# Low weight bits joined as words, bonus rows, copies from two queues, three output tiles: a linear-attention and feed-forward kernel on one core

## Chip, cores, metric

One core of one Trainium2 chip. The metric is the device time of one execution in microseconds (us); the median of three runs of the kernel before is 497.73 us (496.38 to 502.05).

## The reference, cut to what matters

```
# r, k, v: (4, 8, 768, 48);  w, u: (8, 48)
for t in range(768):                       # per batch and head
    y[t]  = r[t] @ (state + outer(u * k[t], v[t]))
    state = w[:, None] * state + outer(k[t], v[t])
x = y, heads side by side                  # 3072 tokens x 384
h = x @ w_in                               # 384 x 2048
out = (h * clip(h + 3, 0, 6) / 6) @ w_out  # 2048 x 384
```

All is float32. The term with `u` (the bonus) acts only between a token and itself.

## The kernel before, in words

The tokens go in chunks of 64 (`C`), with 12 chunks (`NSTEP`) and two halves of the batch-and-head pairs per chunk, so 24 attention steps `i` (`NHALF`). Six groups `g` (`NG`) of 512 columns each hold four attention steps: steps 0 to 3 feed group 0, 4 to 7 group 1, and so on. The feed-forward part runs per group over 16 slices `f` of the hidden width. A unit is one (group, f). Its first half (`ffn1`, line 484; the nine products of `hidden`, line 190) makes a 128x512 tile `h`, which ACT and DVE turn into the activated tile `g` as a high and a low part. Its second half (`ffn2`, line 511; nine products of `project`, line 197) adds to three output banks `o`. Every weight is a pair `w_hi`, `w_lo`, because a product is made of three products of rounded parts.

One attention step (`attention`, line 443) loads `kT`, `rT`, `kt`, `V`, scales keys and queries with powers of `w` (`prepare`: `ks`, `RP`; for steps under `EARLY` = 8 also the elementwise product `X` = `ks` * `RP`), makes the 64x64 scores on PE (`scores`, line 365), puts the bonus on the diagonal of `X` (`put`, line 418) and the masked scores under it (`copy_predicated`, line 441), then on PE the state update (`keep`) and the outputs (`outputs`). A `visit` (line 400) is one block of such small PE products. The state goes through `St` (DVE, line 464) and back into the bank `U` (ACT, line 456). The outputs are split into `x` high (ACT, line 471) and `x` low (DVE, line 472); where a chunk's second half is done, six copies of 32 KB inside on-chip memory (line 479) complete the rows of `x`. Before the change all six are issued by SP.

In steps under 8 the bonus is a product with one column per pair (`self_weight`, line 371): 16 products with `uw` as the single right-hand column, written to column 0 of each score block. `put` then spreads that column over the row. Steps 1 and 3 use output banks 1 and 2 in place of `SC` and `Y` (`where`, line 247). Steps under `APART` have a score visit of their own; later ones share the visit of the step before.

The weights come as 64-bit words (`weights`, line 275), three loads per f into two `raw` buffers in turn. Per f: the upper word is scaled into `z` (line 289 on ACT or 290 on DVE), the low word is rounded by ACT into the low 16 bits of the upper word, in place (line 292, uint32 to uint16, strided), DVE masks sign and three low bits from it (line 293), shifts and joins with `z` (line 295), rounds to `w_hi` (297 ACT or 298 DVE) and subtracts to `w_lo` (line 259).

The three output banks are slices of one tile `ops3`. All instruction orders come from a list scheduler written in the kernel (`Schedule`, line 58): every operation has a cost per engine, its reads and writes by name, and a priority from the longest path behind it; `order` (line 82) picks engine and time. `products` (line 119) also plans instruction fetch in blocks of 256 PE products (`FETCH` us each) and fills idle PE time with products of no use (`warm`, line 615; line 619 in the profile). The constants at lines 41 to 55 are its costs. Engines run their instructions strictly in the emitted order, and the real waits between engines are set from the accesses to tiles. Units go in the order: group 0 f 0 to 5 (`SPLIT`), group 1 whole, group 0 f 6 to 15, groups 2 to 5 whole. The first `CUT` units of group 0 are cut into halves of 256 columns, one per chunk. After group 0's first six, ACT saves the banks to `part` (line 542).

The pages of the profile name fp32 weight loads PEld. `idc` is a 64x64 identity, twice over; `ident` a 128x128 one.

Of the kernel before, what the change touches and what calls it, by code (L numbers as in the profile page):

```python
# [13 lines left out]
U16 = mybir.dt.uint16  # L14
# [27 lines left out]
BEGIN = {"pe": 1.4, "act": 2.1, "dve": 0.9, "pool": 0.8, "sp": 0.8}  # L42
ISSUE, FLIGHT = 0.47, 1.95
QUEUE = 0.3
PIECES = 3
BLOCK, FETCH, FIRST = 256, 4.4, 63
# [3 lines left out]
APART = 5  # L50
SPLIT = 6
LAG = 2
CUT = 1
AHEAD = 4
XBUF = (0, 1, 1, 0, 1, 0)


class Schedule:
# [23 lines left out]
    def order(self):  # L82
# [23 lines left out]

        def run(state, start, count, pace):

            seen, entered = state
            while count:  # L110
                room = BLOCK - seen % BLOCK
                if count < room:
                    return (seen + count, entered), start + count * pace
                start = entered = max(start + room * pace, entered + FETCH)
                seen += room
                count -= room
            return (seen, entered), start

        def products(i, start):

            nonlocal pe
            gap = start - free["pe"] - 0.2
            pace = ops[i][0]["pe"] / ops[i][6]
            busy = [d for d, h in holds.items() if h is None or h + 0.3 > free["pe"]]
            choices = [0]
            if gap > 0.3 and not busy:
                choices = range(int(gap / 0.87) + 1, max(int(gap / 0.87) + 2, int(gap / 0.125)))
            best = None
            for c in choices:
                state, t = run(pe, free["pe"], 4 * c, gap / (4 * c)) if c else (pe, start)  # L130
                state, t = run(state, max(start, t), ops[i][6], pace)
                room = BLOCK - state[0] % BLOCK
                wait = max(0.0, state[1] + FETCH - t - 0.008 * room)
                score = (round(t + 0.5 * wait, 2), c)
                if best is None or score < best[0]:
                    best = score, c, state, t
            _, c, pe, t = best
            if c:
                fills.append((free["pe"] + 0.02, c, gap / c))
            if ops[i][7] is not None:  # L140
                holds[ops[i][7]] = None
            return t
# [3 lines left out]
        while ready:  # L146
            best = None
            for e in free:
                here = [i for i in ready if e in ops[i][0]]
                if not here:  # L150
                    continue
                t = min(begin(i, e) for i in here) + 0.1
                for i in sorted((i for i in here if begin(i, e) <= t), key=lambda i: -prio[i]):
                    start = begin(i, e)
                    end = start + (ISSUE if e == "sp" else ops[i][0][e])
                    if any(begin(i, x) + c < end for x, c in ops[i][0].items() if x != e):
# [6 lines left out]
            if e == "sp":  # L163
                free[e] = start + ISSUE
                line = ready_at = max(line, start + FLIGHT) + ops[i][0][e]
            elif e == "pe":
                free[e] = ready_at = products(i, start)
            else:
                free[e] = ready_at = start + ops[i][0][e]
            if e in ops[i][4]:  # L170
                port = free[e]
            if i in holds:
                holds[i] = free[e]
            done.append((start, free[e], e, i))
            for j in succ[i]:
                for x in at[j]:
                    at[j][x] = max(at[j][x], ready_at + (WAIT[e] if x != e or e == "sp" else 0.03)
                                   + (SPARE.get(e, 0.0) if x != e and ops[j][5] else 0.0))
                waits[j] -= 1
                if not waits[j]:  # L180
                    ready.append(j)
# [22 lines left out]
def fast_path(tc, mp, pp, sb, w_hi, w_lo, b3, wm, badi, hps, ops3, rT, kT, rt, kt, vt, wp, wu, wcat, out):  # L204
# [40 lines left out]
    ops = [ops3[:, m] for m in range(3)]  # L245
# [17 lines left out]
    def load(i):  # L263
        q = i % 2
        for name, dst, src, cost in (("kT", kTt, kT, 0.86), ("rT", rTt, rT, 0.86), ("V", V, vt, 0.74),
# [3 lines left out]
            S.add({"sp": cost}, [], [(name, q)], lambda e, dst=dst, src=src: dma(dst[q], src[i]), LEAD)  # L269
# [5 lines left out]
    def weights(f):  # L275
        for p in range(PIECES):
            cs = slice(NW // PIECES * p, NW // PIECES * (p + 1))
            S.add({"sp": 2.2 / PIECES}, [], [("raw", f % 2, p)], lambda e, cs=cs: dma(raw[f % 2][:, cs], wcat[f][:, cs]))
        words = "p (n two) -> p n two"
        rw, zf, sg = raw[f % 2], z[f % 2], cv[f % 2]  # L280
# [4 lines left out]
        up_b = rw.bitcast(U16).rearrange("p (n four) -> p n four", four=4)[:, :, 2]  # L285
# [6 lines left out]
        S.add({"act": 1.2}, [], [kr + (p,) for p in range(PIECES)], lambda e: act.mul(out=up_b, in_=low, mul=ROUND))  # L292
        S.add({"dve": 0.47}, [kr + (p,) for p in range(PIECES)], [kc], lambda e: dve.tensor_scalar(
            out=sg, in0=up_i, scalar1=-2 ** 31 + 7, scalar2=None, op0=ALU.bitwise_and), port=True)
        S.add({"dve": 0.87}, [kz, kc], [kz], lambda e: dve.scalar_tensor_tensor(  # L295
            out=zi, in0=zi, scalar=3, in1=sg, op0=ALU.logical_shift_left, op1=ALU.bitwise_or), port=True)
# [5 lines left out]
    def consts():  # L302
        def init_pool(e):
            make_identity(nc, ident)
# [5 lines left out]
        S.add({"pool": 1.6}, [], ["ident", "idc"], init_pool, 200)  # L310
# [6 lines left out]
        S.add({"act": 1.0}, ["ident"], ["idc", "mask"], init_mask)  # L317
# [12 lines left out]
        S.add({"pe": 3.1}, ["ident"], ["Y", "o2", "U"], init_rows, 300, count=12)  # L330
# [33 lines left out]
    def scores(i):  # L364
# [8 lines left out]
        work = [score] + [self_weight] * (i < EARLY)  # L373
        return [[functools.partial(fn, n, k) for n in range(2)] for fn in work for k in range(8)], \
            [("ks", q), ("RP", q)] + [("X", q), "uw"] * (i < EARLY), [key]
# [23 lines left out]
    def visit(down, across):  # L399
# [12 lines left out]
        S.add({"pe": 0.25 + 0.11 * max(map(len, one_side))}, list(dict.fromkeys(reads)), list(dict.fromkeys(writes)),  # L412
# [4 lines left out]
    def put(i, bonus, e):  # L417
        eng[e].tensor_tensor(out=X[i % 2], in0=wide(idc), in1=bonus.unsqueeze(2).broadcast_to([128, 8, C]), op=ALU.mult)  # L418
# [17 lines left out]
    def choose(i):  # L436
        q = i % 2
        sc, key = where(i)[0], where(i)[2]
        if i < EARLY:
# [3 lines left out]
    def attention(i):  # L443
# [5 lines left out]
        if i < APART:  # L449
            prepare(i)  # L450
            visit([scores(i)], [])
# [22 lines left out]
        if hf == 1:  # L474
            for n in range(2):
                for j in range(3):
                    r0, d0 = 64 * n + 16 * j, 64 * n + 48
                    S.add({"sp": 0.12}, [("x", XBUF[g], c, b, hl) for b in range(2) for hl in range(2)],
                          [("xh", XBUF[g], c, n, j)], lambda e, j=j, r0=r0, d0=d0: dma(
# [132 lines left out]

    done, fill = S.order()
# [14 lines left out]
def rwkv_ffn_kernel(ctx: ExitStack, tc: tile.TileContext, rT, kT, rt, kt, vt, wp, wu, wcat, ys, out):  # L628
# [13 lines left out]
    ops3 = pp.tile([128, 3, 512], F32, name="o")  # L642
    ops = [ops3[:, m] for m in range(3)]

    with tc.tile_pool(name="main", bufs=1) as mp, tc.manual_schedule():
        fast_path(tc, mp, pp, sb, w_hi, w_lo, b3, wm, badi, hps, ops3, rT, kT, rt, kt, vt, wp, wu, wcat, out)
# [135 lines left out]
```

## Time and profile before

| what | us |
|---|---|
| median of three runs | 497.73 |
| lowest and highest | 496.38, 502.05 |
| the profiled execution, its own time | 497.16 |
| its span, first to last instruction | 495.4 |

The span is 1.76 us shorter than the execution's time. The profile is of one execution. Engines are PE (matrix products), PEld (its weight loads), DVE, ACT, POOL; SPq is the queue engine that issues DMAs. In a list by time each row has its start, its duration, engine, line, tiles and, in brackets, how long the engine was idle before and who released it. The granted clock is a share of full speed.

### The profile page before, as it was taken

The page shows a single profiled execution, that of the slowest core. Times are in us where ns is not written, and L with a number is a line of the kernel's source. Part 1 is how long each engine was busy: PE and PEld are TensorE (multiplying, and loading weights), DVE is VectorE, ACT ScalarE, POOL GpSimd, SP SyncE. Part 2 cuts the span into 40 slices and gives each one's busy share as a digit, 9 for nine tenths or more (in the row PEclk, how much of TensorE's full clock was granted, in tenths as well). Part 3 has the DMA queues.
Part 4 walks back from the last instruction along what each step waited for, and adds up shares of the span by engine and source line. Part 5 has one row for each costly group of instructions (what it writes and reads, how often), then busy time and mean ns, then how long its engine had stood idle before and what let it go on. Part 6 is the DMA issues. An engine that isn't in the chain of part 4 may idle for free.

```text
span 495.4 us, 11559 instructions
## 1 busy us (share of the span) xinstructions
PE 475.2 (96%) x4994; PEld 389.9 (79%) x4994; DVE 295.5 (60%) x475; ACT 197.7 (40%) x289; POOL 38.3 (8%) x40
## 2 busy tenths in 40 slices
PE   8977999799999999999999999999999999999993
PEld 5776877688888888888888788888788888888882
DVE  6786997998574686743566543685543652333331
ACT  2145777787334333333323433343433332433331
POOL 1411310000000111100010000120000100000000
PEclk9887999999999999999999999999999999999998
DMA  8768655456112143330033410143400010100001
GB/s 207 225 168 242 188 154 185 149 179 190 33 53 99 52 121 100 112 110 0 16 115 91 140 28 0 54 129 92 132 3 1 17 34 17 64 1 0 2 0 69
DMA packets 27516, 44.28 MB, mean 89 GB/s; under 512 B 4161, under 2 KB 12482, under 8 KB 27458
## 3 DMA queue, kind: packets, MB, share of 16 engines
q1 hardware_dynamic: 27458, 43.47, 29.5%
q8 instruction: 41, 0.67, 0.6%
q14 instruction: 17, 0.14, 0.1%
HBM read 36.38 MB, written 4.72 MB: 83 GB/s over the span
## 4 chain that ended last, share of the span: by engine, by line
PE 92%; DVE 3%; DMA 2%; issue 1%; ACT 0%; SPq 0%; POOL 0%; DVEq 0%; POOLq 0%
PE o L200 40%; PE h L193 39%; PE Y L362 5%; PE SC L362 2%; PE h L619 2%; PE U L362 2%; PE o L362 1%; DMA x<-x 1%; DMA raw<-wcat 1%; DVE w_lo L259 0%; DVE z L295 0%; PE Y L328 0%; PE o L328 0%; DVE X L418 0%; DVE x L472 0%
## 5 line engine op out<-in xcount | busy, mean ns | idle before, releaser
L200 PE MATMUL o<-g,w_hi 128*128 128x512 f32 (+1 forms) x582 | 195.1, 390 | 4.0 <-ACT part L542 3.2
L193 PE MATMUL h<-x,w_hi 128*128 128x512 f32 (+1 forms) x582 | 164.9, 392 | 4.0 <-DVE t L500 4.0
L500 DVE SCALAR_TENSOR_TENSOR t<-t,h 128x512 f32<-128x512 f32 (+1 forms) x97 | 66.1, 681 | 113.0 <-ACT t L498 112.8
L200 PEld LDWEIGHTS o<-g,w_hi 128*128 128x128 f32 x582 | 108.9, 188 | 29.3 <-ACT part L542 3.7
L193 PEld LDWEIGHTS h<-x,w_hi 128*128 128x128 f32 x582 | 108.1, 188 | 27.2 <-DVE t L500 4.7
L498 ACT ACTIVATE t<-h,b 128x512 f32<-128x512 f32 (+1 forms) x97 | 66.5, 685 | 147.3 <-PE h L193 146.7
L200 PE MATMUL o<-g,w_lo 128*128 128x512 f32 (+1 forms) x291 | 112.7, 387 | 0.0
L259 DVE TENSOR_TENSOR g<-t,g 128x512 fp32r<-128x512 f32 (+1 forms) x97 | 66.4, 685 | 43.2 <-ACT g L504 43.1
L504 ACT CAST g<-t 128x512 fp32r<-128x512 f32 (+1 forms) x97 | 60.3, 621 | 73.4 <-DVE t L500 73.4
L193 PE MATMUL h<-x,w_lo 128*128 128x512 f32 (+1 forms) x291 | 82.0, 390 | 0.0
L193 PEld LDWEIGHTS h<-x,w_lo 128*128 128x128 f32 x291 | 54.6, 189 | 11.7 <-DVE w_lo L259 0.3
L200 PEld LDWEIGHTS o<-g,w_lo 128*128 128x128 f32 x291 | 54.7, 188 | 10.7
L259 POOL TENSOR_TENSOR RP<-rT,E 112x512 f32<-112x512 f32 x16 | 20.2, 1265 | 298.6 <-PE Y L362 272.8
L292 ACT ACTIVATE raw<-raw 128x768 uint16<-128x768 uint32 x16 | 31.3, 1957 | 5.0 <-DVE z L290 4.7
L362 PEld LDWEIGHTS U<-V,KH 64*48 64x48 f32 x704 | 19.1, 128 | 9.5 <-issue 8.3
L362 PE MATMUL SC<-RP,ks 48*64 48x64 f32 x704 | 26.0, 224 | 0.1
L362 PE MATMUL Y<-X,V 64*48 64x64 f32 x704 | 25.7, 226 | 0.0
L362 PEld LDWEIGHTS SC<-RP,ks 48*64 48x64 f32 x704 | 23.1, 137 | 1.7 <-issue 0.6
L362 PE MATMUL U<-V,KH 64*48 64x48 f32 x704 | 21.9, 215 | 2.6 <-issue 1.6
L362 PE MATMUL Y<-RP,St 48*48 48x64 f32 x672 | 24.4, 224 | 0.0
L471 ACT CAST x<-Y 112x512 fp32r<-112x512 f32 x22 | 12.9, 584 | 27.8 <-PE Y L362 27.8
L362 PEld LDWEIGHTS Y<-X,V 64*48 64x48 f32 x704 | 23.2, 128 | 0.0
(83 smaller groups left out, 308.8 us busy)
## 6 DMA issues: line engine op xcount, KB each, us to landing
raw<-wcat SPq DMA_DIRECT2D x48, 256.0 KB, 3.4
kT<-kT SPq DMA_DIRECT2D x24, 224.0 KB, 4.6
rT<-rT SPq DMA_DIRECT2D x24, 224.0 KB, 4.3
kt<-kt SPq DMA_DIRECT2D x24, 192.0 KB, 4.6
V<-vt SPq DMA_DIRECT2D x24, 192.0 KB, 3.2
rt<-rt SPq DMA_DIRECT2D x16, 192.0 KB, 4.5
outT<-cv SPq DMA_DIRECT2D x12, 256.0 KB, 2.1
x<-x SPq DMA_DIRECT2D x72, 32.0 KB, 2.0
```

The costliest lines, as they stand in the source:

```text
L193: nc.tensor.matmul(h, (w_hi, w_lo)[wl][:, f, 0, 128 * j:128 * j + 128], x(j, hl), start=(m == 0 and j == 0), stop=(m == 2 and j == 2))
L200: nc.tensor.matmul(o[m], (w_hi, w_lo)[wl][:, f, 1, 128 * m:128 * m + 128], g(hl), start=(clear and k == 0), stop=(last and k == 2), skip_g ...
L259: emit = lambda e: eng[e].tensor_tensor(out=out, in0=in0, in1=in1, op=op)
L292: S.add({"act": 1.2}, [], [kr + (p,) for p in range(PIECES)], lambda e: act.mul(out=up_b, in_=low, mul=ROUND))
L362: nc.tensor.matmul(out, lhsT, rhs, start=start, stop=True, skip_group_check=True)
L471: S.add({"act": 0.49}, [ky], [kx + (0,)], lambda e: act.copy(out=hi, in_=yt), LEAD)
L498: S.add({"act": 0.13 + 0.23 * ns}, [("h", n % 2), "b3"], [kt_], lambda e: act.activation(out=t[:, :T], in_=h[:, :T], func=AF.Relu, bias=b3 ...
L500: last = S.add({"dve": 0.05 + 0.28 * ns}, [("h", n % 2), kt_], [kt_], lambda e: dve.scalar_tensor_tensor(out=t[:, :T], in0=t[:, :T], scala ...
L504: S.add({"act": 0.08 + 0.22 * ns}, [kt_], [kg + (0,)], lambda e: act.copy(out=gt[:, 0, :T], in_=t[:, :T]))
L619: nc.tensor.matmul(hps[1][:, :cols], ident, rhs, start=True, stop=True)
```

## The change

1. Weights: ACT writes the rounded low word to a separate int32 tile (`cv`, now called `bits`), contiguous. DVE joins sign bit and low bits in one two-input instruction, in place of the one-input mask; the shift and join into `z` follows as before. The planned costs are 0.82 (ACT) for 1.2, and 0.87 (DVE) for 0.47.
2. Bonus in steps 0 to 3: four products per half with `uw` broadcast as 64 weight columns and 128 columns of `X`, into a bank of their own (`h0` for even, `o0` for odd steps); `put` multiplies that bank with the identity. Steps 4 to 7 keep the one-column form.
3. The 12 copies of `x` of group 0 may be issued by ACT or SP, as the scheduler chooses.
4. The scheduler leaves 0.6 us behind a run of fill products (0.2 before), counts them at double length before 7 us, and fetch at 4.9 us per block up to 50 us and 3.9 after (4.4 before). Planned DMA costs rise a little.
5. The output banks are three tiles.
6. `APART` is 4 (5), `CUT` is 2 (1). The set-up of `ident` and `idc` is two operations, `ident` first; the first row products are planned at 5.0 us (3.1).

```
-BEGIN = {"pe": 1.4, ...}
-ISSUE, FLIGHT = 0.47, 1.95
+BEGIN = {"pe": 1.45, ...}
+ISSUE, ISSUE_ACT, FLIGHT = 0.47, 0.65, 1.95
-BLOCK, FETCH, FIRST = 256, 4.4, 63
+BLOCK, FETCH, DENSE, FIRST = 256, (4.9, 3.9), 50.0, 63
+COLD, SLACK = 7.0, 0.6
-APART = 5
+APART = 4
-CUT = 1
+CUT = 2
...
-            gap = start - free["pe"] - 0.2
+            gap = start - free["pe"] - SLACK
+            wide = 1.74 if start < COLD else 0.87
...
+    def bonus_bank(i):
+        bank, key = ((hps[0], ("h", 0)), (ops[0], "o0"))[i % 2]
+        return bank.rearrange("s (k t) -> s k t", t=C), key
...
-        S.add({"act": 1.2}, [], [kr + (p,) ...], lambda e: act.mul(out=up_b, in_=low, mul=ROUND))
-        S.add({"dve": 0.47}, [kr + (p,) ...], [kc], lambda e: dve.tensor_scalar(
-            out=sg, in0=up_i, scalar1=-2 ** 31 + 7, scalar2=None, op0=ALU.bitwise_and), port=True)
+        S.add({"act": 0.82}, [kr + (p,) ...], [kc], lambda e: act.mul(out=bits, in_=low, mul=ROUND))
+        S.add({"dve": 0.87}, [kc] + [kr + (p,) ...], [kc], lambda e: dve.scalar_tensor_tensor(
+            out=bits, in0=up_i, scalar=-2 ** 31, in1=bits, op0=ALU.bitwise_and, op1=ALU.bitwise_or), port=True)
...
+        def self_rows(n, h):
+            mm(bank[TOK[n], 2 * h:2 * h + 2], uw[DIM[n], h:h + 1].broadcast_to([D, C]), X[q][DIM[n], 2 * h:2 * h + 2], h == 0)
+        calls = [(score, k) for k in range(8)]
+        if i < 4:
+            bank, kb = bonus_bank(i)
+            calls += [(self_rows, h) for h in range(4)]
+        elif i < EARLY:
+            calls += [(self_weight, k) for k in range(8)]
...
+        if i < 4:
+            S.add({"dve": 0.60}, [kb, "idc"], [("X", q)], lambda e: put(i, bank, e), LEAD)
...
-                    S.add({"sp": 0.12}, ...
+                    S.add({"sp": 0.12, "act": 0.12} if g < 1 else {"sp": 0.12}, ...
...
-    ops3 = pp.tile([128, 3, 512], F32, name="o")
-    ops = [ops3[:, m] for m in range(3)]
+    ops = [pp.tile([128, 512], F32, name=f"o{m}") for m in range(3)]
```

## Rows read from the trace of the kernel before

**Rows 1.** The page: busy us, share of the span and instructions by engine

```profile
PE 475.2 (96%) x4994; PEld 389.9 (79%) x4994; DVE 295.5 (60%) x475; ACT 197.7 (40%) x289; POOL 38.3 (8%) x40
```

**Rows 2.** PE's waits from 96 us on: engine, line, releaser, total, times, longest

```profile
PE o L200 <- ACT cv L536: 0.7, 1, 0.7
```

**Rows 3.** Products of L193, then L200: length, PE, PEld, clock, DMA, GB/s

```profile
0.00:89.76 89.76, 22.45 (x90) 16.19 (x90) 0.92 0.67 197
...
0.00:89.76 89.76, 14.02 (x64) 10.56 (x64) 0.92 0.67 197
```

**Rows 4.** All engines by stretch: length, PE, PEld, DVE, ACT, POOL, clock, DMA, GB/s

```profile
50.00:60.00 10.00, 10.00 (x347) 9.31 (x347) 9.67 (x16) 7.25 (x9) 4.62 (x3) 0.96 0.68 216
60.00:70.00 10.00, 9.35 (x161) 7.24 (x159) 9.93 (x17) 7.24 (x10) 2.05 (x2) 1.00 0.57 173
```

**Rows 5.** In time, 485 to 490 us: the last three banks

```profile
486.17 0.39 PE L200 MATMUL o<-g,w_hi 128*128 128x512 f32 x1
486.60 0.60 ACT L536 ACTIVATE cv<-o 128x512 f32<-128x512 f32 x1 [3.31 <-PE o L200]
...
487.25 0.50 PE L200 MATMUL o<-g,w_hi 128*128 128x512 f32 x1 [0.69 <-ACT cv L536]
...
488.30 0.69 DVE L537 TENSOR_SCALAR cv<-o 128x512 f32<-128x512 f32 x1 [4.29 <-PE o L200]
489.03 0.60 ACT L536 ACTIVATE z<-o 128x512 f32<-128x512 f32 x1 [1.83 <-DVE cv L537]
```

**Rows 6.** In time, 86 to 90 us: ACT and PE

```profile
88.14 1.57 ACT L542 ACTIVATE part<-o 128x512 f32<-128x512 f32 x3
...
86.12 0.39 PE L193 MATMUL h<-x,w_hi 128*128 128x512 f32 x1
89.76 0.50 PE L200 MATMUL o<-g,w_hi 128*128 128x512 f32 x1 [3.24 <-ACT part L542]
```

**Rows 7.** By form, to 72 us: shapes, count, busy us, mean ns, idle before

```profile
L295 DVE SCALAR_TENSOR_TENSOR z<-z,cv 128x768 int32<-128x768 int32 x6 | 5.7, 956 | 0.1
L293 DVE TENSOR_SCALAR cv<-raw 128x768 int32<-128x768 int32 x6 | 3.9, 655 | 1.9 <-ACT raw L292 1.9
...
L500 DVE SCALAR_TENSOR_TENSOR t<-t,h 128x512 f32<-128x512 f32 x3 | 2.0, 679 | 0.0
...
L500 DVE SCALAR_TENSOR_TENSOR t<-t,h 128x256 f32<-128x256 f32 x2 | 0.8, 416 | 0.0
...
L292 ACT ACTIVATE raw<-raw 128x768 uint16<-128x768 uint32 x7 | 13.6, 1950 | 2.7 <-DVE z L290 2.6
L289 ACT ACTIVATE z<-raw 128x768 f32<-128x768 f32 x6 | 5.4, 906 | 4.2 <-DMA raw<-wcat 2.5 <-DVE w_lo L259 1.6
```

**Rows 8.** PE in time, 7 to 12 us

```profile
7.91 1.46 PE L619 MATMUL h<-ident 128*128 128x356 f32 x4
9.31 1.15 PE L362 MATMUL SC<-RP,ks 48*64 48x64 f32 x32
10.29 1.05 PE L362 MATMUL SC<-uw,X 48*64 48x1 f32 x32
```

**Rows 9.** DVE in time, to 50 us, rows with an idle stretch before them

```profile
11.38 0.69 DVE L418 TENSOR_TENSOR X<-idc,SC 128x512 f32<-128x512 f32 x1 [1.36 <-PE SC L362]
...
24.00 0.69 DVE L472 TENSOR_TENSOR x<-o,x 112x512 fp32r<-112x512 f32 x1 [1.98 <-PE o L362]
...
39.62 0.56 DVE L259 TENSOR_TENSOR KH<-kt,TW 128x384 f32<-128x384 f32 x1 [3.39 <-DMA kt<-kt]
```

**Rows 10.** SP's queue in time: start, us, issues (merged)

```profile
24.72 4.58 SPq L479 DMA_DIRECT2D x<-x  x6
...
34.42 5.72 SPq L479 DMA_DIRECT2D x<-x  x6
```

**Rows 11.** Chain that ended last, in time: the third unit's first half

```profile
46.50 3.59 PE h L193 x9
...
76.31 2.04 PE h L193 x9
```

More of the change, by code (lines that the diff above doesn't have):

```diff
@@ L105, in begin, with takes, late @@
             return max(t, line - FLIGHT - QUEUE) if e == "sp" else t
+        def takes(i, e):
+            return (ISSUE if e == "sp" else ISSUE_ACT) if "sp" in ops[i][0] else ops[i][0][e]
+        def late(t):
+            return FETCH[t > DENSE]
         def run(state, start, count, pace):
@@ L113, in run @@
                     return (seen + count, entered), start + count * pace
-                start = entered = max(start + room * pace, entered + FETCH)
+                start = entered = max(start + room * pace, entered + late(entered))
                 seen += room
@@ L132, in products @@
                 room = BLOCK - state[0] % BLOCK
-                wait = max(0.0, state[1] + FETCH - t - 0.008 * room)
+                wait = max(0.0, state[1] + late(state[1]) - t - 0.008 * room)
                 score = (round(t + 0.5 * wait, 2), c)
@@ L138, in products @@
             if c:
-                fills.append((free["pe"] + 0.02, c, gap / c))
+                fills.append((free["pe"] + 0.02, c, gap / c * 0.87 / wide))
             if ops[i][7] is not None:
@@ L154, in order @@
                     start = begin(i, e)
-                    end = start + (ISSUE if e == "sp" else ops[i][0][e])
-                    if any(begin(i, x) + c < end for x, c in ops[i][0].items() if x != e):
+                    end = start + takes(i, e)
+                    if any(begin(i, x) + takes(i, x) < end for x in ops[i][0] if x != e):
                         continue
@@ L162, in order @@
             ready.remove(i)
-            if e == "sp":
-                free[e] = start + ISSUE
+            if "sp" in ops[i][0]:
+                free[e] = start + takes(i, e)
                 line = ready_at = max(line, start + FLIGHT) + ops[i][0][e]
@@ L316, in init_mask @@
                 act.copy(out=idc[TOK[par]], in_=ident[TOK[par], TOK[par]])
-        S.add({"act": 1.0}, ["ident"], ["idc", "mask"], init_mask)
+        S.add({"act": 0.85}, ["ident", "idc"], ["idc", "mask"], init_mask)
         def init_dve(e):
@@ L397, in outputs, with visit @@
             [("V", q), ("X", q)] + [("St", q), ("RP", q)] * (i > 1), [key]
-    def visit(down, across):
+    def visit(down, across, extra=0.0):
         reads, writes = [], []
@@ L411, in emit @@
                     fn()
-        S.add({"pe": 0.25 + 0.11 * max(map(len, one_side))}, list(dict.fromkeys(reads)), list(dict.fromkeys(writes)),
+        S.add({"pe": 0.25 + 0.11 * max(map(len, one_side)) + extra}, list(dict.fromkeys(reads)), list(dict.fromkeys(writes)),
               emit, LEAD, count=4 * sum(map(len, sum(one_side, []))))
@@ L450, in attention @@
             prepare(i)
-            visit([scores(i)], [])
+            visit([scores(i)], [], 0.44 if i < 4 else 0.0)
             choose(i)
@@ L611, in fast_path @@
                 ffn2(*u, [m])
+    for i, us in SHIFT.items():
+        op = S.ops[i]
+        S.ops[i] = op[:3] + (op[3] + us,) + op[4:]
     done, fill = S.order()
```

48 lines of the change are left out of this document (24 added, 24 removed).

## The prediction

> **What bounds the kernel now.** The page comes first: PE is busy 96% of the span, DVE 60%, ACT 40% [rows 1]. That average hides two regimes, so the next view is PE's waits from 96 us on. There is one, of 0.7 us, in the last microseconds [rows 2]. From there PE runs unit after unit with no gap, and the change takes no product out of a unit. Nothing it does can shorten this part; a microsecond won ahead of it arrives whole at the end.
>
> The third view splits the unit products at 89.76 us, the end of PE's last long wait. Up to there the first halves took 22.45 us of PE and the second halves 14.02 [rows 3]. So 36.5 us of unit work fills a stretch of 89.76. This ramp is where time can be won. In it the table of all engines shows DVE busy 9.67 and 9.93 us of 10 between 50 and 70 us, with ACT at 7.25 and 7.24 [rows 4]. PE seems full there too, but part of that is attention products and fills. DVE is the bound of the late ramp; ahead of it DVE loses time to waits [rows 9]. The last views are the tail in time [rows 5] and the wait at 86 us [rows 6].
>
> The change can thus act in three places: ramp, gap at 86 us, tail. I add three terms to the profiled execution's own 497.16 us (0.57 below the median of the runs, 497.73); the 1.76 us outside the span stay.
>
> **Tail: the three tiles.** The banks are separate, yet their users go strictly one after another [rows 5]. The fourth product from the end, the last of bank 1, starts at 486.17 and ends at 486.56; only then does ACT read bank 0, whose own products ended three products earlier (0.68 us, at the 2.04 us for nine of [rows 11]). PE waits for that read until 487.25 to write bank 2, DVE reads bank 1 only at 488.30, behind PE's writes of bank 2, and ACT reads bank 2 at 489.03, behind DVE. Each waits for a user of another bank, which follows if the waits are set per tile. As three tiles: PE goes on at 486.40 without a wait, three products end at 487.24, ACT reads bank 2 at about 487.28 in place of 489.03. That is 1.75 us. The three output transfers then lie closer together and may slow each other: I bound the gain by 1.0 (the 0.69 us wait of PE and a part of DVE's) and 1.75, and take 1.7.
>
> **Gap at 86 us.** The product that starts at 86.12 is the last before a wait of 3.24 us for ACT's three copies of the banks into `part`, which run 88.14 to 89.71 [rows 6]. With three tiles the first product needs only the first copy, a third of 1.57: 1.04 us less. The rest is ACT being late: the copies stand behind other work in ACT's order. The change takes 1.04 us per weight slice off ACT (below), so the copies may come early enough to hide under the unit half ahead of them. Bounds 0 (the new order has another wait here) and 3.24; I take 2.0, twice the sure part.
>
> **Weights.** ACT's rounding takes 1,950 ns; the scaling of as many elements, also read with a stride but written as contiguous 32-bit words, 906 [rows 7]. That is the nearest row for the new form: −1.04 us of ACT per slice, bounded by 0 if the conversion and not the strided 16-bit write makes it long. On DVE the one-input mask (655 ns on average) becomes a two-input instruction like the shift-and-join, 956 ns: +0.30 us per slice, six slices by 72 us, +1.8 us on the engine that is the bound. In return DVE's waits for ACT's rounding, 1.9 us [rows 7], should mostly go: −1.3 (bounds 0 and 1.9).
>
> **Bonus rows.** Sixteen one-column products per step (32 instructions, 1.05 us) become eight of 128 columns (16 instructions) [rows 8]. They stream as many columns as the score products, 32 instructions of 64 in 1.15 us, so I take +0.1 us per step, bounds −0.5 (half the instructions) and +1.1 (twice the time). DVE's `put` stays one instruction over 128x512. Four steps, beside other waits: 0.
>
> **Start.** The fill at 7.91 lasts 1.46 us, and the first scores begin right behind it, at 9.31 [rows 8]; DVE then waits 1.36 us for them [rows 9]. With the row products planned at 5.0 us and 0.6 us kept free, the planned gap for this fill nearly closes: −1.2 (bounds 0 and 1.36).
>
> **Three tiles in steps 1 and 3.** DVE's low part of `x` for step 1 sat behind 1.98 us of waiting for PE's writes to a bank of `o` [rows 9]. Those writes are the scores of step 3, in another bank than the one it reads. Apart, the low part (0.69 us) and what follows fit into the wait: −1.2 (bounds 0 and 1.98).
>
> **Copies from two queues, `APART`, `CUT`.** SP spent 4.58 and 5.72 us on its two runs of six copies [rows 10], and loads are queued behind them: DVE waits 3.39 us for `kt` [rows 9] in the second. Shared by two queues the runs shrink by 2.3 to 2.9; I take −2.5 from DVE's wait, bounds 0 and −3.39. ACT has room for six issues so early, if it isn't held up (a rival). The Trainium skill, DMA: Bandwidth & Descriptors, section "Issuing engines are not separate DMA queues", speaks against it: transfers from all issuers share the same engines, and only the time to issue is saved, usually small. By that rule the term would be near 0 and the sum 492.0; no row can part issue from waiting inside the merged runs, so I keep to the rows. The joint visit of step 4 saves PE a stretch of small products where DVE is the bound: 0. The additional cut unit costs DVE two half-width instructions for one, 2 x 416 − 679 = 0.15 us [rows 7], twice (`t` and `g`): +0.3.
>
> **Sum.** Ramp: −1.2 − 1.2 − 2.5 − 1.3 + 1.8 + 0.3 = −4.1, rounded to −4.0, because a win at one wait partly shows up at the next. With gap and tail: 497.16 − 4.0 − 2.0 − 1.7 = 489.5 us. What is late next is DVE itself: with its waits gone it has no idle time left between 30 and 70 us.
>
> **Rivals.**
> *DVE takes it back.* If the ramp is DVE's work from end to end, the waits removed early turn up as other waits and the added 2.1 us eat the rest: ramp 0. With the sure part of the gap: 497.16 − 1.0 − 1.7 = 494.5. For it: 9.93 of 10 in 60 to 70 us [rows 4]. Against it: 3.39, 1.98 and 1.36 us of idle DVE ahead [rows 9].
> *ACT relieves DVE.* Freed of 1.04 us per slice, ACT takes the `w_hi` casts that DVE now does. Then the added DVE work is offset (ramp −6 to −7), the whole gap goes (−3.2), and with the tail it is 497.16 − 6.6 − 3.2 − 1.7 = 485.7; down to 484 with the full waits. For it: ACT is a quarter idle in 50 to 70 us [rows 4]. Against it: the scheduler gives a cast to whoever ends it first, which is mostly DVE.
> *Colder PE, slower than before.* Shorter fills and fewer of them leave PE idle longer in front of the ramp's visits and units, and its clock falls from 2.4 to 1.2 GHz. Place: the first units. The row: the third unit's first half took 3.59 us [rows 11], where a later one takes 2.04 [rows 11]. Each such half costs 1.5 us; five of them, and four visits of 64 or more products at 1.7 more each (estimated at the same ratio), make 14: 489.5 + 14 = 503.5. It decides from 8 us on, that is from three cold halves and two cold visits beyond today's. The Trainium skill, TensorE: Matmul & The Clock Gate, section "Why this matters for your kernels", says as much: idle gaps between bursts of products bring the half clock back. Against it: the ramp is already interrupted, and the mean clock to 89.76 us is still 0.92 [rows 3].
> That the tiles don't separate the users, and the tail stays as it is, I count with the first rival (496.2 with ramp 0 and gap 1).
>
> **How the numbers follow.** Forecast 0.48, DVE takes it back 0.24, ACT relieves DVE 0.20, colder PE 0.08. A change of 1% (4.98 us, below 492.75) is about what a measurement of this kernel tells from none. Faster by more: 0.48 + 0.20 = 0.68; within: 0.24; slower: 0.08. The lower end, 484.5, takes nearly all of the good rival; the upper, 495.5, all of the first but its worst corner. The cold case and both edges stay outside, some 2 in 10.
>
> **What would show it.** Tail: no wait of PE for ACT in the last unit, and ACT's read of bank 2 within 0.1 us of PE's last product. Gap: PE's wait for `part` at 2 us or less. Weights: a rounding of about 0.9 us on ACT, the join at 0.96 on DVE. Start: first scores near 8 us. Copies: runs of three on SP, the others on ACT, and no DVE wait over 1 us for `kt`. Ramp: dense units from about 83 us on in place of 89.76. I am wrong if DVE's idle time up to 50 us is no smaller, if ACT is held by its issues while PE waits for it, or if more unit halves take over 3 us.

## The result, and the profile after

| | us |
|---|---|
| kernel before, 9 executions: median (lowest to highest) | 498.75 (495.44 to 502.62) |
| changed kernel, 9 executions: median (lowest to highest) | 493.76 (492.29 to 496.95) |
| ratio with its 95% interval | 0.9889 [0.9847, 0.9932] |
| profiled execution of the changed kernel, its span | 494.05, 492.3 |

The kernel became faster by 1.1%, which is 5.5 us of 498.75 (the two medians differ by 4.99). The ratios here and below leave out executions that took over 1.5% more than the fastest of the same kernel, among them four of the twelve of slack_old (497.64 to 539.85 us). The forecast was 489.5 with a range of 484.5 to 495.5: the median lies inside, 4.3 above the forecast and 0.7 below the 494.5 of the rival "DVE takes it back". Seen as a gain, it is 5.5 where 7.7 were forecast (from 497.16) and 2.7 in that rival.

The profiled executions differ by less, 497.16 − 494.05 = 3.1 us. The one of the kernel before lies 1.6 below the median of the nine. Terms of about a microsecond, read from one profile of each kernel, must be taken with that in mind.

The page after, first part, beside [rows 1]:

```profile
PE 471.2 (96%) x4932; PEld 389.3 (79%) x4932; DVE 305.0 (62%) x479; ACT 183.7 (37%) x293; POOL 34.4 (7%) x36
```

DVE has 9.5 us more work than before, ACT 14.0 less, POOL 3.9 less.

**Where the 3.1 us are.** Both kernels issue the same units in the same order, so the first halves can be laid side by side, counted back from ACT's copies into `part`. First the kernel before, PE in time (three first halves):

```profile
61.02 0.96 PE L193 MATMUL h<-x,w_hi 128*128 128x512 f32 x3 [0.65 <-DVE t L500]
...
67.43 0.98 PE L193 MATMUL h<-x,w_hi 128*128 128x512 f32 x3
...
71.86 0.84 PE L193 MATMUL h<-x,w_hi 128*128 128x512 f32 x3
```

The same three of the changed kernel, then its products and ACT's copies around the place of the old wait:

```profile
60.74 0.96 PE L203 MATMUL h<-x,w_hi 128*128 128x512 f32 x3 [0.20 <-DVE t L525]
...
68.67 0.96 PE L203 MATMUL h<-x,w_hi 128*128 128x512 f32 x3
...
73.86 0.96 PE L203 MATMUL h<-x,w_hi 128*128 128x512 f32 x3 [0.81 <-DVE t L525]
...
87.56 1.56 ACT L567 ACTIVATE part<-o 128x512 f32<-128x512 f32 x3
...
88.35 0.40 PE L210 MATMUL o<-g,w_hi 128*128 128x512 f32 x1
```

From 71.86 (before) and 73.86 (after) on, PE runs a unit every 4.1 to 4.3 us. The changed kernel is 0.28 us ahead at the first of the three, 1.24 behind at the second, 2.00 behind at the third. Then the wait of 3.24 us for `part` [rows 6] is gone: the first product of `o` behind the copies starts at 88.35, not at 89.76. The last part is the tail, in time, beside [rows 5]:

```profile
483.91 0.60 ACT L561 ACTIVATE cv<-o 128x512 f32<-128x512 f32 x1 [2.63 <-PE o L210]
...
484.16 0.62 PE L210 MATMUL o<-g,w_hi 128*128 128x512 f32 x2
...
484.59 0.69 DVE L562 TENSOR_SCALAR cv<-o 128x512 f32<-128x512 f32 x1 [2.59 <-PE o L210]
...
484.84 0.39 PE L210 MATMUL o<-g,w_hi 128*128 128x512 f32 x1
485.27 0.60 ACT L561 ACTIVATE z<-o 128x512 f32<-128x512 f32 x1 [0.76 <-PE o L210]
485.89 0.33 SPq L563 DMA_DIRECT2D outT<-z  x1
```

ACT and DVE read their banks while PE still writes another, PE has no wait, and ACT's last read starts 0.04 us after PE's last product (484.84 + 0.39 = 485.23). The balance of the two spans:

| stretch | before | after | difference |
|---|---|---|---|
| start to the fourth first half ahead of `part` | 71.86 | 73.86 | +2.00 |
| from there to the first `o` product behind `part` | 17.90 | 14.49 | −3.41 |
| from there to the end of the last product | 398.45 | 396.88 | −1.57 |
| from there to the end of the last read | 1.42 | 0.64 | −0.78 |
| from there to the end of the span | 5.77 | 6.43 | +0.66 |
| sum | 495.4 | 492.3 | −3.10 |

Of the −1.57, 0.97 is PE's wait in the tail with the slower products behind it: from the start of the fourth product from the end to the end of the last PE took 2.04 us before (486.17 to 488.21) and takes 1.07 now (484.16 to 485.23). The other 0.60 in 397 us of products has no wait to show for it.

### The profile page after: what moved, and what is told of

Read it like the earlier page. It is cut to its first block, busy times and chain, and to the rows that moved or that the text cites. A ratio compares the mean times of both kernels' runs of the same rounds, so it can differ in the third digit from the quotient of the medians.

```text
span 492.3 us, 11449 instructions
## 1 busy us (share of the span) xinstructions
PE 471.2 (96%) x4932; PEld 389.3 (79%) x4932; DVE 305.0 (62%) x479; ACT 183.7 (37%) x293; POOL 34.4 (7%) x36
## 4 chain that ended last, share of the span: by engine, by line
PE 74%; DVE 13%; DMA 5%; issue 3%; SPq 2%; ACT 1%; ACTq 0%; DVEq 0%
PE o L210 34%; PE h L203 33%; DMA raw<-wcat 4%; PE Y L374 4%; DVE cv L305 2%; PE SC L374 2%; DVE z L307 2%; DVE w_lo L272 1%; DVE g L272 1%; PE U L374 1%; DVE t L525 1%; SPq L504 1%; SPq L291 1%; DVE w_hi L310 1%; DVE RP L272 1%
## 5 line engine op out<-in xcount | busy, mean ns | idle before, releaser
L203 PE MATMUL h<-x,w_hi 128*128 128x512 f32 (+1 forms) x588 | 166.7, 393 | 1.7 <-DVE t L525 1.3
L203 PEld LDWEIGHTS h<-x,w_hi 128*128 128x128 f32 x588 | 109.8, 192 | 24.9 <-DVE t L525 2.9
L210 PEld LDWEIGHTS o<-g,w_hi 128*128 128x128 f32 x588 | 110.6, 189 | 22.6
L203 PEld LDWEIGHTS h<-x,w_lo 128*128 128x128 f32 x294 | 55.6, 192 | 11.7 <-issue 0.5
L374 PE MATMUL Y<-X,V 64*48 64x64 f32 x704 | 24.7, 220 | 0.1
L374 PEld LDWEIGHTS Y<-X,V 64*48 64x48 f32 x704 | 22.2, 123 | 0.2 <-DVE X L466 0.2
L374 PEld LDWEIGHTS Y<-RP,St 48*48 48x48 f32 x672 | 20.7, 123 | 0.8 <-DVE x L497 0.5
```

The costliest lines, as they stand in the source:

```text
L203: nc.tensor.matmul(h, (w_hi, w_lo)[wl][:, f, 0, 128 * j:128 * j + 128], x(j, hl), start=(m == 0 and j == 0), stop=(m == 2 and j == 2))
L210: nc.tensor.matmul(o[m], (w_hi, w_lo)[wl][:, f, 1, 128 * m:128 * m + 128], g(hl), start=(clear and k == 0), stop=(last and k == 2), skip_g ...
L374: nc.tensor.matmul(out, lhsT, rhs, start=start, stop=True, skip_group_check=True)
```

## Experiments

The question was which part brings the 5.5 us, and why the ramp brought none of its 4.

**The tiles alone, and all but the tiles.** The first adds the three tiles to the kernel before, the second takes them from the changed kernel. Neither alters the order of the instructions.

```
# before_three (from the kernel before)
-    ops3 = pp.tile([128, 3, 512], F32, name="o")
-    ops = [ops3[:, m] for m in range(3)]
+    ops = ops3 = [pp.tile([128, 512], F32, name=f"o{m}") for m in range(3)]
# one_bank_tile (from the changed kernel)
-    ops = [pp.tile([128, 512], F32, name=f"o{m}") for m in range(3)]
+    ops3 = pp.tile([128, 3, 512], F32, name="o")
+    ops = [ops3[:, m] for m in range(3)]
```

> The kernel before with the three tiles alone, everything else as it was, the order too. By the tile theory the tail's 1.1 to 1.7 us, 1 to 3 us of the wait at 86 us and about 1 us of step 1's wait are all won by this part: 3 to 5 us below the kernel before, so that three tiles make most of the measured 5 us. Rival, that the other parts carry the win: 1 to 1.5 us below, the tail alone.

> The changed kernel with one thing undone: the three output banks are slices of one tile again. The list scheduler knows the banks by name, so the order of all instructions stays; only waits come back. If waits are set per tile: at the end PE waits about 0.7 us for ACT's read of bank 0, and ACT reads bank 2 more than 1 us behind PE's last product (0.04 us in the changed kernel), +1.1 to +1.7 us; PE waits again for the copies into part, +1 to +3 us; step 1's low part waits for step 3's scores, +1 us. In all 496 to 499 us where the changed kernel has 493.8. Rival, that the hardware orders the readers whatever the tile: no change, 493.8.

Measured: 0.9894 [0.9856, 0.9932] for the tiles alone, 0.9943 [0.9911, 0.9975] for all but the tiles, 0.9889 for both. The tiles alone bring 5.3 us of 498.6, the rest alone 2.8, both together 5.5. Both came out near what the tile theory had expected (3 to 5 us won by the tiles alone; 496 to 499 us without them, where the median was 495.99). The gains don't add: once the tiles are apart, the rest is worth nothing that can be measured. In the profile with one tile the tail has its old form (in time):

```profile
487.56 0.60 ACT L561 ACTIVATE cv<-o 128x512 f32<-128x512 f32 x1 [3.31 <-PE o L210]
...
488.21 0.50 PE L210 MATMUL o<-g,w_hi 128*128 128x512 f32 x1 [0.69 <-ACT cv L561]
...
489.27 0.69 DVE L562 TENSOR_SCALAR cv<-o 128x512 f32<-128x512 f32 x1 [4.29 <-PE o L210]
490.00 0.60 ACT L561 ACTIVATE z<-o 128x512 f32<-128x512 f32 x1 [1.84 <-DVE cv L562]
```

With the tiles alone, the wait for `part` is 0.71 us, not 3.24 (PE and ACT in time):

```profile
87.96 1.57 ACT L542 ACTIVATE part<-o 128x512 f32<-128x512 f32 x3
88.60 0.50 PE L200 MATMUL o<-g,w_hi 128*128 128x512 f32 x1 [0.71 <-ACT part L542]
```

ACT's copies start only 0.18 us earlier than in [rows 6]. PE goes on 0.64 us after their start, behind the first third; before, it went on 1.62 after it, behind all three.

**One part undone at a time.** Each kernel is the changed one with one part taken back; the scheduler then plans the order anew.

```
# weights_old: the one-input mask and the rounding in place
-        S.add({"act": 0.82}, ...
-        S.add({"dve": 0.87}, ...
+        S.add({"act": 1.2}, [], [kr + (p,) for p in range(PIECES)], lambda e: act.mul(out=up_b, in_=low, mul=ROUND))
+        S.add({"dve": 0.47}, [kr + (p,) for p in range(PIECES)], [kc], lambda e: dve.tensor_scalar(
+            out=bits, in0=up_i, scalar1=-2 ** 31 + 7, scalar2=None, op0=ALU.bitwise_and), port=True)
# copies_sp: all copies of x from SP
-                    S.add({"sp": 0.12, "act": 0.12} if g < 1 else {"sp": 0.12}, ...
+                    S.add({"sp": 0.12}, ...
# slack_old
-COLD, SLACK = 7.0, 0.6
+COLD, SLACK = 7.0, 0.2
# apart_cut_old
-APART = 4
+APART = 5
-CUT = 2
+CUT = 1
# bonus_old: one-column products in all eight steps (ROWS = 0)
-        if i < 4:
+        if i < ROWS:
...
```

> The changed kernel with the weights' old form (rounding into 16-bit halves in place, one-input mask). ACT +1.04 us and DVE -0.40 us per slice. My terms for this part were +1.8 for DVE and -1.3 for its waits, so undoing it should be within 1 us of 493.8. Rival, ACT's relief is the win: +3 us or more. Rival, DVE is the bound of the late ramp: -2 to -3 us.

> The changed kernel with all copies of x issued by SP. My term for two queues was 2.5 us: undone, 496 to 496.5 us. Rival, only the time to issue is shared and the transfers share the engines anyway: within 1 us of 493.8. Rival, ACT held by its issues costs as much as SP gains (ACT stood 3.3 us in front of the first rounding and DVE 1.52 us behind it): 0 to 1.5 us below 493.8.

> The changed kernel with 0.2 us kept free behind a run of fills, as before. If overrunning fills delay the visits behind them: +0.5 to +2 us. Rival, the longer fills keep PE's clock up, which stood at 0.50 from 32 to 48 us: 1 to 3 us faster. Rival, neither: within 1 us of 493.8.

> The changed kernel with APART 5 and CUT 1, as before. My terms: 0 for APART, +0.3 for CUT, so within 1 us of 493.8. Fetch theory: step 4's scores are a visit of their own, the same number of instructions in another place, so a stop of 3 to 4 us still comes within 25 to 33 us; where it falls behind the products that DVE waits for, the time is 1 to 3 us less.

> The changed kernel with the one-column bonus in all eight steps. My term for the rows was 0. Fetch theory: 16 more instruction pairs in each of the first four steps, a block of 256 instructions ends half a block earlier by 20 us, and PE's stops for instructions in the first 30 us grow by 1 to 3 us; the clock falls at 13 us as in the kernel before. Then 495 to 497 us. Rival: within 1 us of 493.8.

| kernel | ratio to the kernel before | 95% |
|---|---|---|
| changed | 0.9889 | 0.9847 to 0.9932 |
| weights_old | 0.9886 | 0.9839 to 0.9933 |
| copies_sp | 0.9885 | 0.9852 to 0.9918 |
| slack_old | 0.9891 | 0.9845 to 0.9938 |
| apart_cut_old | 0.9894 | 0.9843 to 0.9944 |
| bonus_old | 0.9894 | 0.9841 to 0.9947 |

The five ratios lie within 0.05 points of the changed kernel's, with half-widths of 0.3 to 0.5%. None shows the 2.5 us (0.5%) that the copies were given, though the two intervals together leave room for about that much; an effect of a microsecond either way stays open. Four expectations were not met: copies_sp did not cost 2 to 2.7 us; slack_old shows none of its 0.5 to 2; bonus_old did not cost the 1 to 3 us of the fetch theory (its stops marked "issue" up to 60 us are 4.3 us in all, the changed kernel's 6.9); and in apart_cut_old the stop between 25 and 33 us is one of 1.48 us, not of 3 to 4. In all four the time is that of the changed kernel, as far as these intervals can tell.

**The stop of PE at 28 us.** The changed kernel shows a wait in the ramp that no dependency explains (PE in time; "issue" means that the profile shows nothing that PE waits for):

```profile
27.41 0.89 PE L374 MATMUL SC<-uw,X 48*64 48x1 f32 x25
32.15 0.37 PE L374 MATMUL SC<-uw,X 48*64 48x1 f32 x3 [3.84 <-issue]
```

Three one-column products of step 4's scores are left when PE stops for 3.84 us. Two theories: PE had run out of fetched instructions, so fewer of them move or remove the stop; or the loads from memory slow their arrival, so lighter loads shorten it. One kernel gives step 4 row products too (16 instructions for 32), another loads only 8 of the words of each weight piece from slice 1 on, with POOL filling the second buffer beforehand.

```
# rows5
-        if i < 4:
+        if i < ROWS:                        # ROWS = 5, in the three places
...
# light_weights
-            cs = slice(NW // PIECES * p, NW // PIECES * (p + 1))
+            cs = slice(NW // PIECES * p, NW // PIECES * (p + 1) if f < 1 else NW // PIECES * p + 8)
...
+            pool.memset(raw[1].bitcast(F32), 1.0)
```

> The changed kernel with the bonus rows for step 4 too: 16 instruction pairs fewer in the visit at 25.6 us, in which PE stood still from 28.31 to 32.15 with three one-column products left. Fetch theory: PE had run out of instructions there; with the visit shorter than what is loaded, the stop falls behind the visit's end, DVE's wait of 3.32 us for these scores goes to under 0.5, and the time falls by 2 to 4 us, to 490 to 492. Rival, DVE's work from end to end sets the ramp: DVE's wait goes, but others take its place and the time stays within 1 us of 493.8. Second rival, a wait on data that the profile doesn't show: PE stands still at the same product as before.

> The changed kernel, same order of all instructions, but the weight loads from slice 1 on bring 8 columns in place of 256 per piece, so all weights but slice 0 are left out of the result; POOL fills the second load buffer once at the start. Traffic theory: PE's stop at 28.31 us is the fetch of instructions held up by data transfers; with less of them it falls from 3.84 us to under 1.5. Rival, the fetch takes its time whatever else is moved: the stop stays between 3 and 4.5 us. Load theory of the ramp: the landing of the weights (7.0 and 6.0 us on the chain) paces it, so the time falls by 3 us or more beyond what the stop gives back, to under 489. DVE theory: the conversions themselves are the pace, 490 to 493.

Measured: rows5 0.9825 [0.9779, 0.9871], light_weights 0.988 [0.9826, 0.9934]. In rows5 the row products of step 4 run through, and DVE needs no wait for them at 29.28; but 4.7 us later DVE waits 3.43 us for ACT, which has waited 6.91 for a weight load (PE, ACT and DVE in time):

```profile
27.56 0.93 PE L375 MATMUL h<-X,uw 48*64 48x128 f32 x14
...
32.58 0.90 ACT L305 ACTIVATE cv<-raw 128x768 int32<-128x768 uint32 x1 [6.91 <-DMA raw<-wcat]
...
33.99 0.69 DVE L498 TENSOR_TENSOR x<-o,x 112x512 fp32r<-112x512 f32 x1 [3.43 <-ACT x L497]
```

In light_weights, with a DMA share of 0.56 where it was 0.75 (28 to 36 us), PE stops ahead of the same three products. So it does in four kernels with full loads, for 4.65 us in one_bank_tile, 2.87 in weights_old, 1.85 in raw3p (below) and 1.79 in copies_sp (PE of light_weights, then of copies_sp):

```profile
31.07 0.89 PE L375 MATMUL SC<-uw,X 48*64 48x1 f32 x25
34.69 0.37 PE L375 MATMUL SC<-uw,X 48*64 48x1 f32 x3 [2.72 <-issue]
```

```profile
29.70 0.28 PE L374 MATMUL SC<-uw,X 48*64 48x1 f32 x3 [1.79 <-issue]
```

Its 2.72 us meet neither theory (under 1.5, or 3 to 4.5). With full loads the length runs from 1.79 to 4.65, and 2.72 lies between: the traces don't show that lighter traffic shortens the stop. They do show what fixes its place. Counted from the start of the trace, 605 products lie ahead of it in all six kernels, at times from 27.9 to 32.0 us. In apart_cut_old, with another order, PE stops behind 605 products too, for 1.48 us ahead of a fill product. In thirteen traces, of the kernel before, the changed kernel and the others (slack_old's left out), 39 stops from 4 to 62 us are marked "issue", and 33 of them lie at counts of the same row: 223 (1.96 us in bonus_old), 349 (0.44 in the changed kernel), 477 (1.64 in the kernel before), 731 (0.99 in rows5), 984 and 1112 (0.29 and 0.22 in the changed kernel). These are 126 to 128 products apart, or twice that. Six stops do not fit, at 617 products in four kernels (1.79 us in the changed one) and at 526 and 982 in one each. With a weight load for each product, 127 products are about 254 instructions, an estimate that lies close to the planner's blocks of 256. So PE stops at certain counts of its own instructions. That supports the fetch theory; that it is the fetch, and what sets the length, stays open.

The load theory was not tested cleanly. POOL's filling of the buffer (1.38 us) lies beside a small DVE operation of the set-up that takes 1.30 us in place of 0.17, the first scores of light_weights start at 7.95, not at 7.32, and this visit comes 3.7 us later. Still the kernel has the same time, with a DMA share of 0.27 in place of 0.57 from 50 to 70 us. That the weight loads pace the ramp was not seen; a gain as large as the late start would be hidden.

**A third load buffer, alone and with rows5; rows5 with all copies on SP.** The space of `part`, free until about 86 us, serves as a third `raw` buffer for slices 0 to 7.

```
# raw3p
+    raw.append(part.rearrange("p a b -> p (a b)").bitcast(I64))
...
+        r = f % 3 if f < 8 else f % 2       # raw[r] in place of raw[f % 2]
```

> The changed kernel with a third load buffer for the weights of slices 0 to 7 (the space of part, which is written later). SP waited 12.2 us in all for DVE to give such a buffer back. If loads are late because buffers come free late: the time falls by 2 to 4 us. Rival, DVE's conversions pace the ramp and an earlier load waits in its buffer: within 1 us of 493.8. Rival, earlier weight loads delay the attention inputs and the instruction fetch: 1 to 3 us slower.

> Bonus rows for step 4 and the third load buffer together. In rows5 (490.2 us) ACT stood 6.9 us in front of a rounding whose load landed late, and DVE 3.4 us behind ACT. If the third buffer brings that load sooner: 486 to 489 us. Rival, that load had its buffer free (slice 1 is the first user) and was late by SP's order: 489 to 491.

> Bonus rows for step 4, and the copies of x by SP alone. If both relieve the same stretch in their own way: 488 to 490 us, below rows5's 490.2. If what rows5 wins is only the stop moved behind the scores, and the copies were not in its way: 490 to 491. Rival, SP's longer runs delay the loads again: 492 to 494.

| | without rows5 | with rows5 |
|---|---|---|
| changed kernel | 0.9889 | 0.9825 [0.9779, 0.9871] |
| third load buffer | 0.9866 [0.9822, 0.991] | 0.981 [0.9768, 0.9853] |
| all copies on SP | 0.9885 [0.9852, 0.9918] | 0.9858 [0.9812, 0.9905] |

The third buffer alone lies within its interval of the changed kernel. Row products in step 4 gain 0.64, 0.56 and 0.27% in the three pairs, 0.5% on average (2.4 us). Each pair by itself has overlapping intervals; that all three have one sign makes a gain likely, and its way through the ramp wasn't found. The pair with the third buffer was run side by side: 490.20 to 493.31 us without row products in step 4, 488.18 to 490.54 with them. The other two came out as their rivals said, rows5_raw3p with 489.93 us (the buffer did not bring the late load sooner) and rows5_copies_sp with 492.65. The best kernel is rows5 with the third buffer: 0.981, a median of 489.93 beside 499.22 for the kernel before.

## Why the prediction was right or wrong

The time lies in the range and the gain is clear of noise, but not by the account that led there. Tail and gap came as forecast in kind; the ramp, 4.0 of the 7.7 us, failed, and the mechanism of the rival "DVE takes it back" stood in its place. That the range held is in part luck: it was drawn wide enough to take that rival in.

**Tail: the reads as worked out, the transfers not counted.** Forecast −1.7 between 1.0 and 1.75. PE's wait and slower products (0.97) and the chain of reads behind the last product (0.78) make 1.75 of gain, exactly as worked out; from the last read to the end of the span 0.66 was lost again. That stretch is 6.43 and 6.33 us in two traces with three tiles (the changed kernel, before_three), 5.77 and 5.90 in two with one tile (the kernel before, one_bank_tile), so the loss goes with the tiles, as the closer output transfers would have it. Net: −1.09, near the lower bound. The prediction had named the cause of that bound and then leaned to the other end.

**Gap: right in kind, larger.** Forecast −2.0; the wait of 3.24 is gone. Three things closed it: PE needs the first copy only (1.04 forecast; 0.98 with the tiles alone, 1.62 − 0.64), ACT's copies start 0.58 earlier, and PE arrives 1.99 later. The third is no gain: it is the loss in the ramp, hidden in the gap. Counted with the ramp, the way to the first `o` product got 1.41 shorter, where 6.0 were forecast.

**Ramp: this step failed.** "Ramp: −1.2 − 1.2 − 2.5 − 1.3 + 1.8 + 0.3 = −4.1" became +2.00 in the profiles. (The tiles alone, with the old order, show 73.21 against 71.86, thus +1.35 with nothing in the ramp that could cost it; of the 2.00 only the part beyond the scatter of executions is to be explained. That the ramp won 4 us is excluded either way: with 4.3 us from gap and tail, 5.5 leave it 1.2, an estimate that sets terms of one profile against medians.) The waits that the terms named did vanish. The first scores start at 7.32, not at 9.31, and the row products follow them (PE in time, beside [rows 8]):

```profile
7.32 1.11 PE L374 MATMUL SC<-RP,ks 48*64 48x64 f32 x32
8.27 1.04 PE L374 MATMUL h<-X,uw 48*64 48x128 f32 x16
```

The waits of 1.36, 1.98 and 3.39 us [rows 9] are gone too. Others stand in their place (DVE in time, the rows up to 50 us with an idle stretch before them, without those of the first 3 us):

```profile
22.96 0.96 DVE L305 SCALAR_TENSOR_TENSOR cv<-raw,cv 128x768 int32<-128x768 int32 x1 [1.52 <-DMA x<-x]
32.56 0.69 DVE L440 TENSOR_TENSOR X<-SC,idc 128x512 f32<-128x512 f32 x1 [3.32 <-PE SC L374]
42.47 0.69 DVE L440 TENSOR_TENSOR X<-SC,idc 128x512 f32<-128x512 f32 x1 [1.43 <-PE SC L374]
49.22 0.69 DVE L272 TENSOR_TENSOR ks<-kT,E 112x512 f32<-112x512 f32 x1 [0.91 <-DMA kT<-kT]
```

The largest is PE's stop at 28 us. Even so DVE was busy 39.61 us of the first 50, against 36.57 before. Most of that is not progress, as the groups by form up to 72 us show (line, engine, tiles, shapes, count, busy us and mean ns, idle before). Of the kernel before:

```profile
L259 DVE TENSOR_TENSOR ks<-kT,E 112x512 f32<-112x512 f32 x4 | 2.7, 687 | 0.0
...
L259 POOL TENSOR_TENSOR ks<-kT,E 112x512 f32<-112x512 f32 x5 | 7.0, 1392 | 17.2 <-PE Y L362 6.5 <-DMA kT<-kT 5.8 <-PE SC L362 2.5
```

Of the changed kernel:

```profile
L272 DVE TENSOR_TENSOR ks<-kT,E 112x512 f32<-112x512 f32 x7 | 5.8, 828 | 0.9 <-DMA kT<-kT 0.9
L305 DVE SCALAR_TENSOR_TENSOR cv<-raw,cv 128x768 int32<-128x768 int32 x6 | 5.7, 951 | 1.5 <-DMA x<-x 1.5
...
L272 POOL TENSOR_TENSOR ks<-kT,E 112x512 f32<-112x512 f32 x2 | 2.4, 1188 | 4.3 <-DMA kT<-kT 4.3
...
L304 ACT ACTIVATE cv<-raw 128x768 int32<-128x768 uint32 x7 | 6.4, 916 | 8.8 <-DMA raw<-wcat 5.6 <-DMA x<-x 3.3
```

The mask costs 5.7 in place of 3.9 us, the +1.8 that were forecast. What the prediction did not see is that the scheduler, offered idle time on DVE, moved three `ks` from POOL to it: 5.8 in place of 2.7 us (one of the seven, at 57.34, took 1.68 us beside an operation of POOL). By 50 us four operations had changed over, two `ks`, one `X` and one `RP` of 0.69 us each; that is 2.7 of the 3.04 us that DVE did more by then. The idle time that the change won early went into work that POOL had done before, and the lead at 61 us is 0.28.

Then it is lost. The next two rows are the stretch from the first to the third of the three first halves shown above, before and after (length, PE, PEld, DVE, ACT, POOL, clock, DMA, GB/s):

```profile
61.02:71.86 10.84, 10.84 (x164) 8.49 (x165) 10.70 (x18) 8.45 (x11) 2.05 (x2) 1.00 0.54 163
```

```profile
60.74:73.86 13.12, 10.00 (x165) 8.14 (x165) 12.91 (x18) 7.15 (x12) 3.21 (x2) 1.00 0.52 161
```

DVE does 18 instructions in both and is full in both, but they take 12.91 us, not 10.70. Two new masks of 0.95 in place of two of 0.55 make 0.8 of the 2.2. The rest is one cast and one subtraction that POOL slows (POOL and DVE in time):

```profile
68.51 2.00 POOL L272 TENSOR_TENSOR rt<-rt,ubt 128x384 f32<-128x384 f32 x1 [10.03 <-DMA ubt<-wu]
69.66 1.26 DVE L310 CAST w_hi<-z 128x768 fp32r<-128x768 f32 x1
70.58 1.21 POOL L272 TENSOR_TENSOR rt<-rt,kt 128x384 f32<-128x384 f32 x1
70.95 1.66 DVE L272 TENSOR_TENSOR w_lo<-z,w_hi 128x768 fp32r<-128x768 f32 x1
```

Elsewhere they take 0.56 and 0.96, so the two lose 1.4. In the kernel before POOL's two operations lay at 66.67 and 67.78, beside DVE work that they did not slow (`w_lo` took 1.83 us beside POOL at 58.53, ahead of this stretch). That agrees with the Trainium skill (Advanced Engine Details and Errata, "Mode Summary"), which says that DVE's second port is shared with GpSimd and that instructions which need it block each other.

POOL's two operations start only at 68.51, where 1.52 of the 2.28 us between the leads of 0.28 and −2.00 were already lost. Ahead of that PE waits 1.96 us for the state, because DVE's `St` stands behind the conversion of a weight slice; before, it stood ahead of it (DVE and PE of the changed kernel, then DVE of the kernel before):

```profile
64.94 0.55 DVE L489 TENSOR_TENSOR St<-U,E 112x384 f32<-112x384 f32 x1
...
66.11 0.29 PE L374 MATMUL U<-V,KH 64*48 64x48 f32 x4 [1.96 <-ACT U L481]
```

```profile
61.48 0.55 DVE L464 TENSOR_TENSOR St<-U,E 112x384 f32<-112x384 f32 x1
```

So there was no idle time to win from 61 us on, neither on DVE nor on PE, which before the change was busy 10.84 us of the 10.84. In the changed kernel the stretch is DVE's, and the new mask, the new order and POOL cost 2.2 us: the rival "DVE takes it back". Its mechanism is what the trace shows, but its gap was too small (1.0), and in place of the whole added work (2.1) only the two masks in this stretch weighed, beside things that it did not name, the moved `ks`, the late `St` and POOL's collisions. This is read from one trace of each kernel, and no run changes one of them alone.

One experiment comes near. In apart_cut_old, whose order is planned anew, POOL does nothing in this stretch and `St` comes at 60.33. The next two rows are its stretch from the first to the third of the first halves (columns as above) and its first `o` product behind `part`:

```profile
59.05:70.79 11.74, 10.58 (x166) 8.36 (x164) 11.64 (x18) 6.03 (x10) 0.00 (x0) 1.00 0.63 199
```

```profile
87.22 0.50 PE L210 MATMUL o<-g,w_hi 128*128 128x512 f32 x1 [1.81 <-ACT part L567]
```

It takes 11.74 us in place of 13.12, the two masks' 0.8 over the 10.84 of before still in it, and the third first half comes at 70.79, 1.07 ahead of the kernel before. Then PE waits 1.81 us for `part`, and the time is that of the changed kernel (0.9894). copies_sp is alike: 70.74, and a wait of 1.28 us for `part`. A lead out of the ramp is possible, then, but most of it ends in the gap.

**Copies from two queues: wrong, −2.5 was 0.** SP's runs did shrink, to 3.05 us for three (from 4.58 for six) and 2.41 for four, and DVE's wait for `kt` went. But it went in copies_sp as well, with two runs of six on SP (4.36 and 4.49 us), so the second queue is not what removed it. And ACT paid (SP's queue, ACT's queue and ACT in time):

```profile
19.42 3.05 SPq L504 DMA_DIRECT2D x<-x  x3
...
19.42 2.22 ACTq L504 DMA_DIRECT2D x<-x  x3
22.02 0.90 ACT L304 ACTIVATE cv<-raw 128x768 int32<-128x768 uint32 x1 [3.26 <-DMA x<-x]
```

ACT does nothing for 3.26 us, and DVE's wait of 1.52 at 22.96 stands behind it: the join reads what ACT's rounding writes from 22.02 to 22.92. copies_sp has the time of the changed kernel (0.9885 and 0.9889). The rule that the prediction set against its own term (the Trainium skill, DMA: Bandwidth & Descriptors, "Issuing engines are not separate DMA queues") would make the term near 0, and the runs agree with it. The prediction had let the merged stretches stand as if they delayed everything behind them.

**Weights: sizes right, worth nothing.** ACT's rounding takes 916 ns (906 forecast), the join 951 (956). The 1.04 us per slice that ACT won had no taker: weights_old is as fast. Of DVE's 1.9 us of waiting for the rounding, which were to shrink by 1.3, 1.52 stayed: the wait at 22.96, behind ACT's issues.

**Bonus rows: right.** 16 products of 128 columns take 1.04 us, 32 of one column took 1.05 [rows 8]; undone, the time is the same.

**Colder PE: seen, the damage not measured.** The clock fell to 0.50 (1.2 GHz) within PE's idle 3.84 us and stayed there to 48 us, as in this window (columns as above):

```profile
32.00:36.00 4.00, 2.59 (x12) 2.28 (x12) 3.44 (x6) 0.05 (x1) 0.00 (x0) 0.50 0.46 121
```

The rival put such damage at 14 us. What reached DVE of it is at most its wait of 1.43 us for PE at 42.47; behind that no row shows DVE waiting for PE up to 50 us. PE itself was busy 13.68 of the 15.85 us from 32.15 to 48.00 at this clock, and what that cost its units no run separates. The sign that the prediction named, more unit halves over 3 us, did not come.

**Reading the page.** "36.5 us of unit work fills a stretch of 89.76" took 89.76 for the end of the ramp. But from 46.50 us to the gap PE stood idle for 0.65 us in all (the kernel before, columns as above):

```profile
46.50:86.51 40.01, 39.36 (x583) 31.87 (x583) 35.64 (x56) 29.60 (x35) 6.67 (x5) 0.96 0.61 187
```

Its last fill product starts before 42 us, so "part of that is attention products and fills" misread 50 to 70 us: PE was full there with work that has to be done. A win had to come from ahead of 46.50. Ramp and gap were two limits in a row, the first set by PE and DVE, the second by the tile and ACT; a win in the ramp would have waited in the gap unless both went.

## What to carry to other kernels

Make banks that different engines use at the same time tiles of their own: this edit of two lines alone brought as much as the whole change (0.9894 and 0.9889). Waits removed ahead of a stretch in which another engine is full are not won; look for idle time of PE there first, take the other engine's busy time in that stretch, add what the change and the planner put on it, and let that cap the sum. And compare two traces at the same unit in several places along the ramp: where a lead melts is where the bound is.

## What was not expected of the hardware

PE stopped for 1.79 to 4.65 us in the middle of a run of ready one-column products, in six kernels behind the same 605 products; shorter stops with no releaser stand in the ramp of the kernel before as well (1.6 us behind 477 products, 0.8 behind 350). The counts lie 126 to 128 products apart. A one-column fp32 product costs about as much as one of 64 columns (32 of each take 1.05 [rows 8] and 1.11 us), one of 128 columns twice that (16 in 1.04).
